# Batch 0's token sums by plain loads and three additions, its values in the input's order of heads, and a new table of ranks

## The chip, the cores and the metric

The kernel runs on one core of one Trainium2 chip. The metric is the device time of one execution in microseconds (us). The kernel before took 570.07 us, the median of three runs (569.68 to 573.22). The engines are named as the profile names them: PE multiplies matrices, PEld is its loading of weights, DVE is the vector engine, ACT the scalar engine, POOL the third one (GpSimd), SP issues most of the transfers between HBM and the core's memory.

## The reference

Inputs q, k and v have 8 batches, 8 heads, 576 tokens and 64 values per head. Each head's attention is the sum of two parts; its output goes, heads side by side, as x of [576, 512] per batch into a gated network. The core of it:

```python
q_d = q.reshape(B, H, Sd, factor, D).mean(axis=3)      # factor 4, k_d and v_d alike
out_up = np.repeat(sm_attn(q_d, k_d, v_d), factor, axis=2)
mask = np.abs(pos[:, None] - pos[None, :]) < factor
out_local = np.matmul(softmax(np.where(mask, scores, -1e9)), v)
x = out_up + out_local
h = np.maximum(x @ w_in, 0.0)
u, v = h[..., :d_ff // 2], h[..., d_ff // 2:]
v_n = (v - mu) / np.sqrt(var + 1e-06)
v_s = np.einsum('ts,bsd->btd', w_spatial, v_n) + b_spatial[None, :, None]
return (u * v_s) @ w_out
```

## The kernel before, in words

**Attention.** A batch has four pairs of heads; 32 pairs in all. Each pair goes through two attentions. The local one works in ten windows of 64 tokens: scores S on PE (line 873; on some pairs PE also adds the mask, line 866, on the others DVE does, line 886), maximum (889, or 895 where the mask is in already), subtraction (892 or 901), exponential on ACT (937), total (904), inverse (907, 908), multiplication by it ("norm", 941, on DVE or POOL), transposes T on PE (949), and AV, the product with the values (1060). The other one works on sums of four neighbouring tokens: two sums of q and k (844 and 847, on DVE or POOL), scores Sd (920), maximum, exponential, norm (974), transposes Td, and AVd (1040 for batch 0, 1049 for the others), the product with the token sums of v. The two are added into x (1070, 1072).

**The token sums of v.** The host lays v out as four quarters per batch, each 72 partitions by 1024 floats, one for each place in a group of four tokens. `load_down` loads the first quarter by SP (761) into the tile "tv" and lets POOL issue three transfers that add the others in memory (763).

**The values.** `load_v` loads a pair's ten windows in three transfers (775 and twice 777): the even blocks as they are, the odd blocks with the two heads swapped between the halves of the partitions. So in odd blocks the rows of a head lie in the other half, and in `views` and `values` the pieces of odd blocks are taken crosswise (`r = h ^ (blk % 2)`). AV's output rows always lie in the head's own half.

**The network.** Batch 0 (`FULL = 1`, "whole") is multiplied in plain 32-bit form, with the weights made from their 64-bit bits on DVE (lines 626 to 641; tiles mba to mbd for V, mbe to mbh for U); the other batches as pairs of 16-bit numbers, high and low part. Per batch: five V pieces (PE, line 1125 for batch 0, 1129 after that), then relu, statistics, scaling and the split into "vh"; eight U pieces (1191, 1196); a bound over U (`bound`: a transpose at line 569, the maximum on DVE at 572, a matmul at 575 that spreads it, the scale on DVE at 580 to 586); the spatial product SP with the split w_spatial (1218), the gate on DVE (1235), and the product O with w_out (1255). Each spatial product waits for the matmul that spreads the bound of U (`after=[known]`).

**The scale of w_spatial.** SP loads its rows first (611), ACT takes absolute values and row sums (724), PE adds the columns (740), DVE takes the maximum over the columns (743, tile "sw"), and the scale follows; the split of w_spatial and the scales of U come from it.

**What sets the order.** Every piece of work is an operation of the class `Plan`, with an engine, an estimated duration, the tiles that it reads and writes and a rank from the table ORDER. `Plan.run` walks through time and, for the engine that is free first, takes among the operations that can start within NEAR nanoseconds the one of lowest rank (PE keeps its tile shape where the rank is at most STAY behind). `Way` with the strings of ON says which engine does a kind of operation for each pair. Each engine then runs its list strictly in order, and so does each engine's queue of transfers. `warm` puts idle matmuls (1306) where PE would stand idle in the first 110 us.

Of the kernel before, what the change touches and what calls it, by code (L numbers as in the profile page):

```python
# [1351 lines left out]
```

## Time and profile before

| what | value |
|---|---|
| median of three runs | 570.07 us (569.68 to 573.22) |
| profiled execution | 572.09 us, span 570.3 us, mean granted clock 0.976 |
| PE busy | 547.1 us (96%) |
| DVE busy | 449.1 us (79%) |
| ACT busy | 358.5 us (63%) |
| POOL busy | 139.0 us (24%) |
| chain that ended last | PE 82%, DVE 10%, DMA 4%, ACT 2% |
| batch 0: first whole V, first spatial product | 53.64 us, 99.37 us |
| batch 1: first split V | 132.56 us |

The span is the time from the first to the last instruction of the profiled execution, and 1.79 us lie around it; this execution was 2.02 us above the median. The busy share is a mean over stages with different limits, so what an engine is worth has to be read by stage: the beginning, in which inputs come in and batch 0's attention runs on its own; batch 0's network beside batch 1's attention; and then the even part, in which each batch's network runs beside the next batch's attention. A duration in a row is that of one instruction, or of several that overlap (x2, x40), and an idle time in brackets is what its engine waited before it.

### The profile page before, as it was taken

How to read it: one execution, taken by the hardware profiler on the slowest of the kernel's cores; microseconds unless marked ns; L12 is line 12 of the kernel's file. 1: busy time of each engine (PE TensorE's matmuls, PEld its weight loads, DVE VectorE, ACT ScalarE, POOL GpSimd, SP SyncE). 2: the span in 40 equal slices, each digit the busy share in tenths (PEclk: the TensorE clock that was granted, in tenths of full speed). 3: DMA queues.
4: the chain of work that ended last, by engine and by line, in shares of the span. 5: the costliest groups of instructions: out<-in, count | busy, mean ns of one | idle time of the engine just before them, and what ended most of it. 6: DMA issues, size and time to landing. Idle time of an engine off the chain costs nothing.

```text
span 570.3 us, 15614 instructions
## 1 busy us (share of the span) xinstructions
PE 547.1 (96%) x6307; PEld 368.4 (65%) x6307; DVE 449.1 (79%) x1227; ACT 358.5 (63%) x913; POOL 139.0 (24%) x162
## 2 busy tenths in 40 slices
PE   5778799999999999999999999999999999999997
PEld 3446357866677567766678566766767756766573
DVE  5899989997989679886789798898969787832550
ACT  3758777765875578555766776657675666544422
POOL 4414331211421224101520054001610162001400
PEclk9758999999999999999999999999999999999999
DMA  9999834214550444415432336332450301000102
GB/s 241 264 259 285 196 66 120 94 35 142 105 144 25 148 99 96 124 38 173 69 105 70 127 93 135 109 113 87 109 139 8 114 33 39 21 1 18 50 7 92
DMA packets 40467, 59.76 MB, mean 105 GB/s; under 512 B 4042, under 2 KB 27210, under 8 KB 40396
## 3 DMA queue, kind: packets, MB, share of 16 engines
q1 hardware_dynamic: 38092, 51.69, 31.3%
q0 software_dynamic: 2304, 7.08, 7.6%
q8 instruction: 49, 0.80, 0.6%
q14 instruction: 22, 0.18, 0.1%
HBM read 46.57 MB, written 9.44 MB: 98 GB/s over the span
## 4 chain that ended last, share of the span: by engine, by line
PE 82%; DVE 10%; DMA 4%; ACT 2%; issue 1%; SPq 0%; POOL 0%; DVEq 0%; POOLq 0%; ACTq 0%
PE pma L1255 5%; PE pmc L1255 5%; PE pmd L1218 4%; PE pma L1196 4%; PE pma L1218 4%; PE pmb L1218 4%; PE pmc L1218 4%; PE pmb L1196 4%; PE pma L1129 4%; PE pmc L1129 4%; PE pmd L1255 3%; PE pmb L1255 3%; PE pmd L1129 3%; PE pmb L1129 3%; PE pmd L1196 3%; PE paa L1060 2%
## 5 line engine op out<-in xcount | busy, mean ns | idle before, releaser
L1218 PEld LDWEIGHTS <-vha 128*128 128x128 f16 x768 | 73.6, 98 | 19.5
L1196 PEld LDWEIGHTS <-win 128*128 128x128 f16 x672 | 64.8, 98 | 18.4
L941 POOL TENSOR_TENSOR sb<-sb,smb 128x640 f32<-128x640 f32 x12 | 16.4, 1366 | 74.3 <-DVE smb L908 63.9
L1255 PEld LDWEIGHTS <-more 128*128 128x128 f16 x192 | 18.5, 98 | 20.8
L1255 PEld LDWEIGHTS <-g 128*128 128x128 f16 x192 | 18.3, 98 | 20.8
L1218 PE MATMUL pmd<-wsp,vha 128*128 128x320 f16 (+1 forms) x192 | 27.5, 292 | 0.0
L1218 PE MATMUL pma<-wsp,vha 128*128 128x256 f16 (+1 forms) x192 | 26.2, 286 | 0.0
L1160 POOL TENSOR_TENSOR stb<-stb,mhalf 128x1 f32<-128x1 f32 (+1 forms) x13 | 9.7, 743 | 67.3 <-DVE stb L1141 67.3
L1218 PE MATMUL pmb<-wsp,vha 128*128 128x256 f16 (+1 forms) x192 | 25.5, 282 | 0.0
L1218 PE MATMUL pmc<-wsp,vha 128*128 128x256 f16 (+1 forms) x192 | 25.5, 282 | 0.0
L941 POOL TENSOR_TENSOR sa<-sa,sma 128x640 f32<-128x640 f32 x7 | 9.3, 1334 | 48.3 <-DVE sma L908 42.5
L1160 POOL TENSOR_TENSOR stc<-stc,mhalf 128x1 f32<-128x1 f32 (+1 forms) x13 | 9.2, 707 | 45.8 <-DVE stc L1141 45.7
L1255 PE MATMUL pmc<-wo,g 128*128 128x512 f16 x72 | 16.5, 379 | 0.0
L1160 POOL TENSOR_TENSOR sta<-sta,mhalf 128x1 f32<-128x1 f32 (+1 forms) x14 | 9.5, 681 | 26.7 <-DVE sta L1141 24.8
L978 DVE SCALAR_TENSOR_TENSOR eh<-eda,smda,eh 128x144 f16<-128x144 f32 x42 | 15.8, 440 | 0.1
L763 POOL DMA_DIRECT2D tv<-v_dram x12 | 11.5, 955 | 16.4 <-DMA tv<-v_dram 16.4
L1129 PEld LDWEIGHTS <-xa 128*128 128x128 f16 x84 | 8.2, 98 | 9.9
L904 DVE TENSOR_REDUCE smb<-sb 128x10 f32<-128x640 f32 x16 | 12.9, 809 | 1.3 <-ACT sb L937 1.3
L844 POOL TENSOR_TENSOR suma<-qka 128x576 f32<-128x576 f32 x5 | 6.8, 1370 | 29.1 <-DVE sma L904 16.9
L937 ACT ACTIVATE sb<-sb 128x640 f32<-128x640 f32 x16 | 11.8, 735 | 3.3 <-DVE sb L901 3.1
L1255 PE MATMUL pma<-wo,more 128*128 128x512 f16 x60 | 13.8, 379 | 0.0
L1255 PE MATMUL pmc<-wo,more 128*128 128x512 f16 x60 | 13.8, 379 | 0.0
(1025 smaller groups left out, 1719.7 us busy)
## 6 DMA issues: line engine op xcount, KB each, us to landing
qka<-qk_dram SPq DMA_DIRECT2D x16, 576.0 KB
qkb<-qk_dram SPq DMA_DIRECT2D x16, 576.0 KB, 5.1
tv<-v_dram POOLq DMA_DIRECT2D x12, 288.0 KB, 5.9
wst<-v_dram POOLq DMA_DIRECT2D x12, 288.0 KB, 4.6
stg<-w_in_dram SPq DMA_DIRECT2D x6, 512.0 KB, 6.1
out_dram<-rowb SPq DMA_DIRECT2D x8, 256.0 KB, 2.4
out_dram<-rowe SPq DMA_DIRECT2D x7, 256.0 KB
out_dram<-rowa SPq DMA_DIRECT2D x7, 256.0 KB
```

The source lines that it names most:

```text
L763: plan.op("POOL", 850, lambda r=r: nc.gpsimd.dma_start(t.ap, v4[b, r], accum_op=ALU.add), w=[t], rank=rank + 2.0 + 0.3 * r, kb=288, name="tv")
L844: side(s1).tensor_tensor(sb.ap.rearrange("p x (g r) -> p x g r", r=2), x[:, :, :, :2], x[:, :, :, 2:], op=ALU.add)
L904: nc.vector.tensor_reduce(sm.ap, s.ap, axis=AX.X, op=ALU.add)
L937: exp_of.append(plan.op("ACT", 643, lambda: nc.scalar.activation(s.ap, s.ap, AF.Exp, scale=1.0 / 8.0), w=[s], rank=R["E"], name="exp"))
L941: plan.op(nm, 0, lambda: side(nm).tensor_tensor(s.ap, s.ap, sm.ap[:, :, None].broadcast_to([P, NW, 64]), op=ALU.mult), r=[sm], w=[s], rank ...
L978: nc.vector.scalar_tensor_tensor(eh.ap[:, a, :, 1], ed.ap[:, a, :], smd.ap[:, a:a + 1], eh.ap[:, a, :, 0], op0=ALU.mult, op1=ALU.subtract)
L1060: nc.tensor.matmul(pv.ap[h * 64:h * 64 + 64, c:c + QB[w + 1] - QB[w]], vb.ap[k, w], pT.ap[k, blk, q0:q0 + QB[w + 1] - QB[w]], start=True, ...
L1129: nc.tensor.matmul(ps.ap, xs[c].ap[:, i, t * P:(t + 1) * P], win[:, c, j, FF:], start=(c == 0 and (i, j) == (0, 0)), stop=(c == NC - 1 and ...
L1160: plan.op("POOL", 830, lambda: nc.gpsimd.tensor_tensor(st.ap[:r, 8:9], st.ap[:r, 8:9], mhalf[:r], op=ALU.pow), w=[st], rank=rank - EVICT, ...
L1196: nc.tensor.matmul(ps.ap[:, :n], win[:, c, i, ft * P:(ft + 1) * P], xs[c].ap[:, j, HA[h]:HA[h + 1]], start=(c == 0 and (i, j) == (0, 0)), ...
L1218: nc.tensor.matmul(ps.ap[:, :n], vh.ap[:, c, i, fs], wsp[:, c, j, hs], start=(c == 0 and (i, j) == (0, 0)), stop=False)
L1255: nc.tensor.matmul(ps.ap, g.ap[:, c, i, k:k + P] if t < NT else gt.ap[:, c, i], wo[:, c, j, :], start=(c == 0 and (i, j) == (0, 0)), stop= ...
```

## The change

Three things change for batch 0, and the order of everything.

The token sums of batch 0: the four quarters are loaded by SP with plain transfers into storage that batch 0's network uses only later (two into the tile "vh", two into the nine tiles "us"), and three additions of 72x1024 make the sum, two on DVE and one on POOL. The other batches keep the adding transfers.

The values of batch 0: one transfer per pair, heads unswapped. `views` and `values` take odd blocks straight where the batch is whole. Each head's rows then lie in the same half at AV's input and output.

The table ORDER is replaced (some 1,600 numbers), with NEAR 121 for 131.8 and STAY 12.56 for 5.08, and the strings of ON: among others one "shrink" of the weights more on DVE, more early masks on PE (letters T), other places for sums and norms. The durations that the planner counts with change to 450 for a load of batch 0's values and 1150 for an AV of batch 0.

```diff
-    583.50, 595.07, 582.09, 590.75, 523.79, 633.37, 571.27]
-NEAR = 131.8
-STAY = 5.08
+    548.47, 513.63, 618.17, 559.57]
+NEAR = 121
+STAY = 12.56
...
-ON = {"shrink": "AAAAAAADA",
-      "sum": "DPDPDPDDPDDDPDPDDPDDDDDDPDDDPDDP",
-      "mask": "DDDTTTDTDDTTDTDDDDTTDTDDDDDDTD",
+ON = {"shrink": "AAADAAADA",
+      "vsum": "DDP",
+      "sum": "DPPPDPDDDDDDPDPDDPPDDDDDDDPDPDDP",
+      "mask": "DTTTTTTTDDTDDTDDDDTTDTDTDDDDTD",
...
-    places("u", 9, [P, HN], F32)
+    us = const.tile([P, 9, HN], F32, name="us")
+    plan.tag("u", [us[:, i] for i in range(9)])
+    quarters = [a[:72, i * 2 * FF:(i + 1) * 2 * FF].rearrange("p (j d) -> p j d", j=NP)
+                for a in (vh.rearrange("p t i f -> p (t i f)").bitcast(F32), us.rearrange("p i t -> p (i t)")) for i in range(2)]
...
     def load_down(b):
+        if b < FULL:
+            for r in range(4):
+                plan.op("SP", 450, lambda r=r: nc.sync.dma_start(quarters[r], v4[b, r]), w=[("v4", r)], rank=0.0, kb=288, name="v4")
+            for i, (x, y) in enumerate(((0, 1), (2, 3), (0, 2))):
+                w = Way("vsum", i, P=("POOL", 2200, True), D=("DVE", 1135, True))
+                plan.op(w, 0, lambda w=w, x=x, y=y: side(w).tensor_tensor(quarters[x], quarters[x], quarters[y], op=ALU.add),
+                        r=[("v4", y)], w=[("v4", x)], rank=RANK["th"][0], name="vsum")
+            tv_of[b] = None
+            return
...
+            if b < FULL:
+                nc.sync.dma_start(vb.ap, vw[b, p])
+                return
...
-            sv = s.ap.rearrange("p (j h) k -> p h j k", h=2)[:, ::-1 if odd else 1, odd::2]
+            sv = s.ap.rearrange("p (j h) k -> p h j k", h=2)[:, ::-1 if odd and not whole else 1, odd::2]
...
-                r = h ^ (blk % 2)
+                r = h if whole else h ^ (blk % 2)
...
-            av = plan.op("PE", 675, values, r=[vb, pT], w=[pv], hold=[xf, x], after=after, rank=R["AV"], lag=PEL, mode="Q", name="AV")
+            av = plan.op("PE", 1150 if whole else 675, values, r=[vb, pT], w=[pv], hold=[xf, x], after=after, rank=R["AV"], lag=PEL, mode="Q", name="AV")
```

Three places of the order. First DVE ahead of the maximum over the columns of w_spatial (the tiles s and mx are scores and their maxima, ed and md belong to the attention on sums). Before:

```order
L925 TENSOR_SCALAR mxdb<-mxdb 128x3
L974 TENSOR_TENSOR eda<-eda,smda 128x432
L889 TENSOR_REDUCE mxb<-sb 128x10
L904 TENSOR_REDUCE sma<-sa 128x10
L892 TENSOR_TENSOR sb<-sb,mxb 128x640
L907 TENSOR_SCALAR sma<-sma 128x10
L908 RECIPROCAL sma<-sma 128x10
L961 TENSOR_SCALAR smdb<-smdb 128x3
L962 RECIPROCAL smdb<-smdb 128x3
L904 TENSOR_REDUCE smb<-sb 128x10
L907 TENSOR_SCALAR smb<-smb 128x10
L908 RECIPROCAL smb<-smb 128x10
L743 TENSOR_REDUCE sw<-pma 128x1
```

and now, where vh and us are the quarters:

```order
L907 TENSOR_REDUCE mxa<-sa 128x10
L913 TENSOR_REDUCE mxb<-pab 128x10
L919 TENSOR_TENSOR sb<-pab,mxb 128x2x3x64
L919 TENSOR_TENSOR sb<-pab,mxb 128x2x2x64
L910 TENSOR_TENSOR sa<-sa,mxa 128x640
L770 TENSOR_TENSOR vh<-vh 72x1024
L770 TENSOR_TENSOR us<-us 72x1024
L941 TENSOR_REDUCE mxdb<-pmd 128x2
L942 TENSOR_REDUCE mxdb<-pmb 128x1
L943 TENSOR_SCALAR mxdb<-mxdb 128x3
L922 TENSOR_REDUCE sma<-sa 128x10
L922 TENSOR_REDUCE smb<-sb 128x10
```

Two additions of quarters, and the maximum and subtraction of the second pair straight from its scores, which carry the mask already, now stand there; the maximum over the columns (750) comes ten rows later.

Second SP's queue at the start (qk are q and k of a pair, wst the rows of w_spatial, va to vd the values). Before:

```order
L837 DMA qka<-qk_dram 128x1152
L837 DMA qkb<-qk_dram 128x1152
L611 DMA xfa<-bsp_dram 2x576
L761 DMA tv_125<-v_dram 72x1024
L611 DMA wst<-wT_dram 128x576 x4
L611 DMA wst<-wT_dram 64x576 x2
L775 DMA va<-vw_dram 128x3x128
L777 DMA va<-vw_dram 64x2x128 x2
L837 DMA qka<-qk_dram 128x1152
L775 DMA vb<-vw_dram 128x3x128
L777 DMA vb<-vw_dram 64x2x128 x2
```

and now:

```order
L855 DMA qka<-qk_dram 128x1152
L855 DMA qkb<-qk_dram 128x1152
L767 DMA vh<-v_dram 72x1024
L618 DMA xfa<-bsp_dram 2x576
L767 DMA vh<-v_dram 72x1024
L767 DMA us<-v_dram 72x1024 x2
L618 DMA wst<-wT_dram 128x576 x4
L618 DMA wst<-wT_dram 64x576 x2
L855 DMA qka<-qk_dram 128x1152
L791 DMA va<-vw_dram 128x640
L791 DMA vb<-vw_dram 128x640
L791 DMA vc<-vw_dram 128x640
L791 DMA vd<-vw_dram 128x640
L618 DMA stg<-w_in_dram 128x1024 x2
L855 DMA qkb<-qk_dram 128x1152
```

Four quarters stand ahead of w_spatial where one stood; the values take one issue each and come one behind another, ahead of w_in (stg) and of the next q and k.

Third PE between the last U piece and the first spatial product of batch 0 (the rows that load weights of the ident and cross matrices are left aside). Before:

```order
L1191 MATMUL pma<-xd,mbh 128x320
L569 MATMUL pmd<-ident,sw 4x128
L873 MATMUL pab<-qka 64x64 x20
L575 MATMUL pmd<-sw,one 128x1
L569 MATMUL pmc<-ident,uta 8x128
L866 MATMUL paa<-mask_b,mask_a 64x320
L873 MATMUL paa<-qkb 64x64 x20
L1049 MATMUL pma<-pdTa,th_126 64x144
L575 MATMUL pmc<-uta,one 128x1
```

and now:

```order
L1209 MATMUL pmb<-xd,mbh 128x320
L576 MATMUL pma<-ident,sw 4x128
L1067 MATMUL pmc<-pdTa,th_126 64x144
L576 MATMUL pmd<-ident,uta 8x128
L582 MATMUL pma<-sw,one 128x1
L967 MATMUL pab<-ident,sa 128x128 x5
L938 MATMUL pmb<-kdb 64x144 x2
L938 MATMUL pmc<-kdb 64x144 x2
L938 MATMUL pmb<-kdb 64x144 x2
L582 MATMUL pmd<-uta,one 128x1
L1078 MATMUL paa<-probTb,vf 64x60 x2
L1236 MATMUL pma<-wsp,vh 128x256
```

A transpose of probabilities (967), an Sd (938) and half an AV (1078) now stand ahead of the first spatial product, with two spreads of maxima (582) between them.

## Rows read from the trace of the kernel before

**Rows 1.** The page: busy time of each engine (first row), and the span in 40 equal slices, each digit the busy share of PE in tenths; DMA is the mean busy share of the 16 DMA engines in the same slices:

```profile
PE 547.1 (96%) x6307; PEld 368.4 (65%) x6307; DVE 449.1 (79%) x1227; ACT 358.5 (63%) x913; POOL 139.0 (24%) x162
...
PE   5778799999999999999999999999999999999997
...
DMA  9999834214550444415432336332450301000102
```

**Rows 2.** The windows by stage: start and end, length, then busy time (and instructions) of PE, PEld, DVE, ACT and POOL, PE's granted clock, the DMA share and GB/s:

```profile
0.00:20.00 20.00, 12.78 (x138) 7.25 (x139) 12.38 (x32) 9.47 (x29) 10.49 (x32) 0.89 0.98 240
20.00:53.40 33.40, 26.23 (x463) 18.79 (x461) 31.76 (x74) 24.84 (x64) 9.71 (x10) 0.71 1.01 275
53.40:99.37 45.97, 41.83 (x249) 24.52 (x249) 43.01 (x117) 34.32 (x88) 13.36 (x14) 0.96 0.59 135
99.37:132.56 33.19, 33.19 (x449) 23.17 (x446) 31.49 (x96) 24.01 (x58) 5.18 (x4) 1.00 0.31 97
132.56:571.00 438.44, 433.02 (x5017) 294.70 (x5015) 330.48 (x912) 265.81 (x675) 100.24 (x103) 1.00 0.31 83
```

**Rows 3.** The timeline of PE: start, duration, engine, line and operation, out<-in with shapes, how many run together, and in brackets the idle time before and what ended it:

```profile
53.64 1.02 PE L1125 MATMUL pmd<-mba,xa 128*128 128x512 f32 x2
...
68.76 0.77 PE L949 MATMUL paa<-ident,sb 128*128 128x128 f32 x5 [3.59 <-POOL sb L941]
...
70.09 2.07 PE L1125 MATMUL pmb<-mba,xa 128*128 128x512 f32 x2
...
99.37 1.48 PE L1218 MATMUL pmd<-wsp,vha 128*128 128x256 f16 x12
...
132.56 0.81 PE L1129 MATMUL pmc<-win,xe 128*128 128x512 f16 x3
```

**Rows 4.** The timeline of DVE, the same columns:

```profile
19.20 0.46 DVE L743 TENSOR_REDUCE sw<-pma 128x1 f32<-128x288 f32 x1
...
45.90 0.82 DVE L895 TENSOR_REDUCE mxa<-pab 128x10 f32<-128x640 f32 x1 [0.51 <-PE pab L873]
46.82 0.89 DVE L901 TENSOR_TENSOR sa<-pab,mxa 128x384 f32<-128x384 f32 x2
...
52.58 0.70 DVE L1070 TENSOR_TENSOR xd<-pab,dnb 128x232 f32<-128x232 f32 x2
...
71.67 0.74 DVE L602 SCALAR_TENSOR_TENSOR win<-mba,sw,win 128x512 f16<-128x512 f32 x1
...
75.59 0.28 DVE L572 TENSOR_REDUCE sw<-pmc 4x1 bf16<-4x128 f32 x1 [0.92 <-PE pmc L569]
...
95.40 0.28 DVE L572 TENSOR_REDUCE sw<-pmd 4x1 bf16<-4x128 f32 x1 [0.43 <-PE pmd L569]
...
97.22 0.86 DVE L886 TENSOR_TENSOR sa<-pab,mask 128x384 f32<-128x384 f32 x2
98.00 0.27 DVE L572 TENSOR_REDUCE uta<-pmc 8x1 bf16<-8x128 f32 x1
98.20 0.80 DVE L889 TENSOR_REDUCE mxa<-sa 128x10 f32<-128x640 f32 x1
```

**Rows 5.** The adding transfers of batch 0 on POOL in the timeline, then the landing times of line L763 up to 36 us, then the first AVd on PE in the timeline:

```profile
9.11 1.02 POOL L763 DMA_DIRECT2D tv<-v_dram  x1 [1.69 <-DMA tv<-v_dram]
...
27.08 0.84 POOL L763 DMA_DIRECT2D tv<-v_dram  x1 [0.56 <-DMA tv<-v_dram]
...
DMA to landing us min/median/max: 7.2/8.1/8.8
...
37.13 0.76 PE L1040 MATMUL pmd<-pdTa,tv 72*64 72x144 f32 x4
```

**Rows 6.** The timeline of POOL (one row) and of DVE: instructions alone and beside POOL:

```profile
19.26 1.54 POOL L941 TENSOR_TENSOR sb<-sb,smb 128x640 f32<-128x640 f32 x1
...
20.04 1.39 DVE L844 TENSOR_TENSOR suma<-qka 128x576 f32<-128x576 f32 x1 [0.19 <-DMA qka<-qk_dram]
...
43.13 0.75 DVE L844 TENSOR_TENSOR suma<-qka 128x576 f32<-128x576 f32 x1
43.79 0.16 DVE L961 TENSOR_SCALAR smdb<-smdb 128x3 f32<-128x3 f32 x1
...
44.08 0.43 DVE L847 TENSOR_TENSOR kda<-suma 128x288 f32<-128x288 f32 x1
...
95.98 1.12 DVE L961 TENSOR_SCALAR smda<-smda 128x3 f32<-128x3 f32 x1
...
99.60 0.81 DVE L892 TENSOR_TENSOR sa<-sa,mxa 128x640 f32<-128x640 f32 x1
```

**Rows 7.** The timeline of SP's queue (issues of transfers, the duration is that of issuing) and one row of ACT:

```profile
2.36 4.25 SPq L611 DMA_DIRECT2D wst<-wT_dram  x6
...
8.81 1.31 SPq L777 DMA_DIRECT2D va<-vw_dram  x2
...
22.05 1.07 SPq L611 DMA_DIRECT2D stg<-w_in_dram  x2
...
12.04 0.68 ACT L724 ACTIVATE wsp<-wst 128x576 bf16<-128x576 f32 x1
```

**Rows 8.** The timeline of PE: AV of the first pair and the larger piece of the last pair of batch 0:

```profile
21.70 1.11 PE L1060 MATMUL paa<-probTa,va 64*64 64x60 f32 x40
...
50.57 0.81 PE L1060 MATMUL pab<-probTb,vd 64*64 64x60 f32 x38
```

More of the change, by code (lines that the diff above doesn't have):

```diff
@@ L61, in __init__ @@
     def __init__(self, kind, i, **ways):
-        s = ON[kind]
+        s = ON.get(kind, "D")
         self.kind, self.i, self.ways = kind, i, ways
@@ L422 @@
 MB = 8
-ON = {"shrink": "AAAAAAADA",
-      "sum": "DPDPDPDDPDDDPDPDDPDDDDDDPDDDPDDP",
-      "mask": "DDDTTTDTDDTTDTDDDDTTDTDDDDDDTD",
-      "norm": "PPPPDPPPDPDPPDDDDPPDDPDPDPDDP",
-      "normd": "DPPAPAAADPAPAAAPPADAAPDADAAADDDA",
-      "vlo": "DPDDDPDDDDDPDPDDPDPDPDPPDPDPPDPPDDDP"}
+ON = {"shrink": "AAADAAADA",
+      "vsum": "DDP",
+      "sum": "DPPPDPDDDDDDPDPDDPPDDDDDDDPDPDDP",
+      "mask": "DTTTTTTTDDTDDTDDDDTTDTDTDDDDTD",
+      "norm": "PPPPDPPPDPDDDDDPDDDPDPDPPPDPPD",
+      "normd": "DPPAPAAAAPAAPAAPAADADADAAADDDA",
+      "vlo": "DPDDDPPDDDDPPDDDPPPDPPDPDDPPDDPPPDDPPDP"}
 @with_exitstack
@@ L537, in tile_kernel @@
     places("xtail", 2, [P, NC, 2, TAIL], F16)
-    places("vh", 1, [P, NT, 2, FF], F16)
+    vh = const.tile([P, NT, 2, FF], F16, name="vh")
+    plan.tag("vh", [vh])
     places("vt", 1, [P, FF], F16)
@@ L757, in load_down @@
     def load_down(b):
+        if b < FULL:
[7 more added lines that the diff above has]
+            return
         t = tv_of[b] = plan.buf("tv")
         rank = NP * b + RANK["tv"][min(b, 2)]
-        plan.op("SP", 450, lambda: nc.sync.dma_start(t.ap, v4[b, 0]), w=[t], after=exp_of[NP * b - NP + 1:][:1] if b else (), rank=rank, kb=288, name="tv0")
+        plan.op("SP", 450, lambda: nc.sync.dma_start(t.ap, v4[b, 0]), w=[t], after=exp_of[NP * b - NP + 1:][:1], rank=rank, kb=288, name="tv0")
         for r in range(1, 4):
@@ L777, in go @@
                 nc.sync.dma_start(dst[(1 - h) * 64:(2 - h) * 64, 1::2], src[h * 64:h * 64 + 64, 1::2])
-        plan.op("SP", 1500, go, w=[vb], after=exp_of[NP * b - NP + p:][:1] if b else (), rank=NP * b + 0.2 * p + RANK["vload"][min(b, 2)], kb=320, name="v")
+        plan.op("SP", 450 if b < FULL else 1500, go, w=[vb], after=exp_of[NP * b - NP + p:][:1] if b else (), rank=NP * b + 0.2 * p + RANK["vload"][min(b, 2)], kb=320, name="v")
         if b < FULL:
@@ L1039, in values_d @@
                 for kc, n in enumerate(KEYS):
-                    nc.tensor.matmul(pw.ap[h * 64:h * 64 + 64, :G], tv.ap[:, p, (2 * kc + h) * D:(2 * kc + h + 1) * D], t[:n, kc, :, h, :],
+                    nc.tensor.matmul(pw.ap[h * 64:h * 64 + 64, :G], quarters[0][:, p, (2 * kc + h) * D:(2 * kc + h + 1) * D], t[:n, kc, :, h, :],
                                      start=(kc == 0), stop=(kc == 1))
@@ L1075, in finish @@
         def finish(*after):
-            av = plan.op("PE", 675, values, r=[vb, pT], w=[pv], hold=[xf, x], after=after, rank=R["AV"], lag=PEL, mode="Q", name="AV")
+            av = plan.op("PE", 1150 if whole else 675, values, r=[vb, pT], w=[pv], hold=[xf, x], after=after, rank=R["AV"], lag=PEL, mode="Q", name="AV")
             avd = plan.op("PE", 450 if whole else 240, values_d if whole else values_h,
-                          r=[*((tv,) if whole else (th_of[b].sub(0),)), pdT.sub(0), pdT.sub(1)], w=[pw], hold=[dn], after=[av] if after else (), rank=R["AVd"], lag=PEL, mode="H", name="AVd")
+                          r=[*((("v4", 0),) if whole else (th_of[b].sub(0),)), pdT.sub(0), pdT.sub(1)], w=[pw], hold=[dn], after=[av] if after else (), rank=R["AVd"], lag=PEL, mode="H", name="AVd")
             if after:
```

242 rows, old and new, of the table ORDER are left out of this document.

## The prediction

> **What bounds the kernel now.** I read the page first, then the windows by stage, then the timeline of PE and DVE. PE is busy for 547.1 of 570.3 us, and its 40 slices show where the rest went: the first four [rows 1]. The windows [rows 2] say it in numbers. From 132.56 us on, PE works 433.02 of 438.44 us at a granted clock of 1.00, so nothing but PE counts there. From 20 to 53.4 us it works 26.23 of 33.40 at a clock of 0.71, and DVE 31.76: here DVE is the engine that has no room. From 53.4 to 99.37 (the first matmul of the spatial product) DVE works 43.01 of 45.97, PE 41.83. So from about 20 us to the first spatial matmul DVE's order sets the pace; from there on PE does; the first whole V of batch 0 is at 53.64, the first spatial product at 99.37, the first split V of batch 1 at 132.56 [rows 3].
>
> The profiled execution took 572.09 us, span 570.3 and 1.79 around it; the median of three is 570.07, that is 2.02 less. I work on the profiled times and take 2.02 off at the end.
>
> **What is removed.** The chain for batch 0's token sums: one SP load, then three adding transfers issued by POOL, the first at 9.11 and the last at 27.08, each waiting for the one before, which land 7.2 to 8.8 us after issue; the first AVd can start at 37.13 [rows 5]. Three issues of 0.84 to 1.02 us leave POOL, which had 9.71 us of work in 33.4 [rows 2]: worth nothing there. That x of the first head pair now comes some 9 us earlier is also worth nothing by itself, since DVE went on with other work meanwhile (31.76 of 33.40).
>
> **What is added.** (1) Three quarters more at the head of SP's queue, 72x1024 floats each, 0.885 MB in all. At 240 GB/s, the rate of the first window [rows 2], that puts the weights of the spatial product, issued behind them (2.36 in [rows 7]), up to 3.7 us later. ACT's absolute-value passes over them begin at 12.04, column sums on PE follow, and DVE's maximum over these is at 19.20 [rows 4, 7]. Between the passes and the maximum lies other work of ACT and PE that need not wait with them, so I take 2.2 of the 3.7: the maximum at 21.4. Bounds: 0.9 (the DVE work newly ahead of it) and 3.7.
> (2) Three additions of 72x1024, two on DVE and one on POOL. On DVE 128x576 takes 0.75 and 128x640 0.81 [rows 6]; the slope gives 1.15 for 1024, in proportion it is 1.30. I take 1.14 each, 2.3 together. On POOL 128x640 took 1.54 [rows 6]: 2.2 to 2.5 for the one. POOL's own time is free.
> (3) Values in one transfer per head pair, where SP issued three, 1.31 us for the latter two [rows 7]. The DMA engines are full there (0.98, 1.01 in [rows 2]), so SP's issue time is not what is short: nothing.
> (4) Batch 0's AV without the swap of heads in odd blocks. Rows of AV are 1.11 us early and, at the full clock, 0.81 [rows 8]. PE idles 7.2 us in that window, and before the last x (DVE, 52.58) its AV (50.57 to 51.38) has 1.2 us to spare: nothing, if an AV grows by less than that. Beside this stands the Trainium skill, "TensorEngine Tiling (Array Packing)", Tile-to-Partition Mapping: a 64x64 tile is fixed by its input half and its output half, four in all, so that heads never swapped use two of the four; AV would take up to twice as long, and with 0.8 us on the path the gain would be 0.3 us instead of what follows.
>
> **What moves.** The table of ranks lays all engines anew. Steady state has PE work alone, with the same instructions, and it cannot gain: 0, with 1 us either way. What counts is the road to the first spatial matmul.
> On DVE I take the maximum for the bound of batch 0's U (on "uta", 98.00 in [rows 4]) as the mark, since the spatial products wait for the matmul that spreads it; the first follows it by 1.37 us. By the order printed above, ahead of it now stand two token additions (+2.3), four more maxima on scores that carry the mask already (4 x 0.82) and their subtractions (4 x 0.89 the pair), for three fewer masks (3 x 0.86), two fewer maxima over a masked tile (2 x 0.80) and subtractions (2 x 0.81), one total (0.80, as a maximum) and the larger part of one x (0.70) more, one weight product (0.74) and one second sum (0.43) less [rows 4, 6]; small pieces come to some 0.6 more. That is 4.3 by durations; consecutive starts lie some 0.08 closer than durations, so 4.0.
> Against it, waits that DVE had and whose cause goes: 0.64 where a sum ran beside POOL's normalization (1.39 against 0.75 [rows 6]), 0.96 on a 128x3 instruction (1.12 against 0.16 [rows 6]), 0.51, 0.92 and 0.43 for PE [rows 4]. Together 3.46, for places that the new order takes apart. New is the later maximum at the start, 2.2 less the 0.9 of work: 1.3. So the mark comes at 98.00 + 4.0 - 3.46 + 1.3 = 99.9 and the first spatial matmul at 101.3.
> Then PE: of what lay between it and the first split V, one T (0.77 [rows 3]), one AV (0.81 [rows 8]), one AVd (0.7 as four matmuls of it in [rows 5]) and one Sd (0.5, estimated from its share of these) now stand ahead of it, 2.8, and some 0.2 for changes between tile shapes. 33.2 becomes 30.2, the split V starts at 131.5 and not 132.56. The gain is 1.1 us: 572.09 - 1.1 = 571.0, less 2.02: **569.0 us**.
> That PE itself does not stop it: with the first whole V at 56.4 instead of 53.64 (one more head's scores, mask, T and AV lie ahead, 2.3, and the sign pass of the first weight block 0.5 later), without the 3.59 us hole at 68.76 and with the V pieces behind it as fast as at 53.64 (two in 1.02, and not in 2.07; the next two alike, 1.8 in all) [rows 3], plus 1.2 of moved pieces, PE would be there at 98.0. It waits for DVE there, late in U's bound.
>
> **The rivals.**
> - *PE alone sets the start* (faster). If DVE loses 3 us less than I think (of the 12.2 it idles up to 99.37 [rows 2]), the spatial product starts at 98.0, the split V at 128.2: 4.4 gained, **565.7**; with the tail 1 us better, 564.7. For it: the hole at 68.76 was a wait for POOL, which the new order puts elsewhere. Against it: 4 us more DVE work on that road.
> - *The parked maximum* (slower). DVE runs in order, and behind the maximum stand all its score passes. If the quarters cost the full 3.7 us and none of the 3.46 us of old waits is won back, the mark is at 98.0 + 4.0 + (3.7 - 0.9) = 104.8, the split V at 136.4, 3.8 later: **573.9**. It decides against the change as soon as DVE loses 1.1 us more than in my sum, since that is the whole gain. For it: DMA is full for 50 us [rows 1], and the later weights w_in (issued 22.05 [rows 7]) queue behind the same bytes. Against it: the three adding transfers moved the same 0.885 MB before 35 us.
> - *POOL's addition holds DVE.* The row: a DVE sum that began beside POOL's normalization ended 0.6 us after it (19.26+1.54 = 20.80; 20.04+1.39 = 21.43 [rows 6]), as if it had begun at its end. POOL's 72x1024 addition may so cost DVE up to its own 2.2 us: 569.0 + 2.2 = **571.2**. The Trainium skill, "SBUF — State Buffer", Who interferes with whom, has this as a rule (two inputs in SBUF against a POOL instruction that reads SBUF: the later one is blocked until the end); these rows agree.
> - *Nothing moves*: the start is absorbed where DMA is full and both orders reach 132.56 alike: **570.1**.
>
> **How the numbers follow.** Forecast 0.45 (568 to 570.5 with its small terms), PE alone 0.22, the parked maximum 0.15, POOL's hold 0.10, nothing moves 0.08. The range takes in PE alone and the parked maximum up to its full price, and leaves out mixtures beyond: 564.0 to 574.0. One per cent, about what a measurement here can tell, is 5.7 us: 564.4 and 575.8. Below the first lies the better half of "PE alone" with a better tail or a second hole closed, 0.13; above the second the parked maximum with w_in late as well, 0.06; between them 0.81.
>
> **What would show it.** Right: AVd of the first pair before 30 us; the columns' maximum near 21.4; first whole V near 56.4 with no hole of over 2 us behind it; first spatial matmul near 101.3 with PE waiting for DVE just before; the first split V near 131.5; no change from there to the end. PE alone would show as a spatial start near 98 with DVE early. The parked maximum would show as DVE idle for 3 us or more ahead of it, and the first whole V past 58; POOL's hold as a DVE row of over 2 us beside the addition. The prediction is wrong if the steady part is not of equal length, since I gave the table of ranks no effect there.

## The result and the profile after

The changed kernel took 576.00 us, the median of five executions (575.86 to 576.43), against 570.07 before (569.68 to 573.22): 1.0087 of the time before, 95% interval 1.0065 to 1.0109. It is slower, by 3.7 to 6.2 us. The profiled execution took 575.86 us, span 573.7, 0.14 below its median; the one of before had been 2.02 above its own, so the two profiles lie only 3.8 us apart.

The windows of the changed kernel, with the same borders as [rows 2] (the last one is longer by 4 us):

```profile
0.00:20.00 20.00, 10.06 (x132) 5.25 (x133) 13.98 (x28) 8.93 (x26) 9.38 (x29) 0.93 0.92 288
20.00:53.40 33.40, 25.59 (x383) 19.01 (x382) 27.00 (x67) 21.87 (x61) 15.05 (x15) 0.78 0.79 226
53.40:99.37 45.97, 41.73 (x378) 25.19 (x378) 45.11 (x118) 35.31 (x86) 11.87 (x12) 1.00 0.68 183
99.37:132.56 33.19, 32.57 (x404) 22.98 (x403) 32.23 (x103) 24.05 (x65) 4.66 (x4) 1.00 0.14 39
132.56:575.00 442.44, 436.54 (x5033) 296.16 (x5030) 326.64 (x914) 271.07 (x688) 95.11 (x101) 1.00 0.31 83
```

From 20 to 53.4 us DVE now works 27.00 us where it had 31.76. That is the window in which it had no room, and it now has 6.4 us without work.

PE's timeline: AV of the last pair, the first whole V, the first piece of the fourth, the spread ahead of the spatial product, that product, the first split V:

```profile
54.41 1.30 PE L1078 MATMUL paa<-probTb,vd 64*64 64x60 f32 x38
...
62.22 1.12 PE L1143 MATMUL pmb<-mba,xa 128*128 128x512 f32 x2
...
76.62 1.13 PE L1143 MATMUL pmb<-mba,xa 128*128 128x512 f32 x2 [1.37 <-ACT rowd L1165]
...
103.68 0.16 PE L582 MATMUL pma<-sw,one 4*128 4x1 bf16 x1 [0.54 <-DVE sw L579]
...
106.05 1.16 PE L1236 MATMUL pma<-wsp,vh 128*128 128x256 f16 x9
...
135.86 0.81 PE L1147 MATMUL pmc<-win,xe 128*128 128x512 f16 x3
```

The first whole V is 8.6 us later than in [rows 3] (62.22 for 53.64), the first spatial product 6.7 us (106.05 for 99.37), the first split V 3.3 us (135.86 for 132.56). From there to the end of the span it is 437.8 us, and before it was 437.7. All of the loss arises ahead of the first spatial product, and PE gives half of it back between that and the split V. PE's last wait before that product is for DVE (0.54 <-DVE at 103.68).

DVE's timeline, with the two additions (12.13, 13.26), the column maximum (24.02), the last sign pass over V's weights (61.03) and the mark (104.35), and POOL's timeline beside it:

```profile
12.13 1.22 DVE L770 TENSOR_TENSOR vh<-vh 72x1024 f32<-72x1024 f32 x1
13.26 1.21 DVE L770 TENSOR_TENSOR us<-us 72x1024 f32<-72x1024 f32 x1
...
15.09 1.83 DVE L943 TENSOR_SCALAR mxdb<-mxdb 128x3 f32<-128x3 f32 x1
...
19.34 1.23 DVE L979 TENSOR_SCALAR smdb<-smdb 128x3 f32<-128x3 f32 x1
...
24.02 0.46 DVE L750 TENSOR_REDUCE sw<-pmd 128x1 f32<-128x288 f32 x1 [2.93 <-PE pmd L747]
...
25.50 0.16 DVE L587 COPY sw<-pma 128x1 f32<-128x1 f32 x1 [0.84 <-PE pma L582]
...
27.02 0.82 DVE L913 TENSOR_REDUCE mxb<-paa 128x10 f32<-128x640 f32 x1 [0.74 <-PE paa L891]
...
48.74 0.46 DVE L941 TENSOR_REDUCE mxda<-pmc 128x2 f32<-128x288 f32 x1 [1.11 <-PE pmc L938]
...
49.45 1.61 DVE L943 TENSOR_SCALAR mxda<-mxda 128x3 f32<-128x3 f32 x1
...
61.03 0.67 DVE L648 SCALAR_TENSOR_TENSOR mbd<-rowc,mbd 128x512 int32<-128x512 int32 x1
...
104.35 0.27 DVE L579 TENSOR_REDUCE uta<-pmd 8x1 bf16<-8x128 f32 x1
```

```profile
14.56 2.34 POOL L770 TENSOR_TENSOR vh<-vh,us 72x1024 f32<-72x1024 f32 x1 [5.99 <-DVE us L770]
19.11 1.44 POOL L959 TENSOR_TENSOR sa<-sa,sma 128x640 f32<-128x640 f32 x1 [2.21 <-DVE sma L926]
...
49.58 1.45 POOL L862 TENSOR_TENSOR suma<-qkb 128x576 f32<-128x576 f32 x1
```

Three things are to be read here. The column maximum came at 24.02 us where it had been at 19.20 [rows 4], after 2.93 us of waiting for PE, and 0.84 and 0.74 us follow. Second, instructions on 128x3 that take 0.16 us elsewhere [rows 6] took 1.83, 1.23 and 1.61 us. Each ends with a POOL instruction: 15.09+1.83 = 16.92 and 14.56+2.34 = 16.90; 19.34+1.23 = 20.57 and 19.11+1.44 = 20.55; 49.45+1.61 = 51.06 and 49.58+1.45 = 51.03. In the last of the three, DVE's row begins 0.13 us before POOL's and is held all the same. Third, the addition on POOL is the longest of these. Behind its victim, the scaled maximum "mxdb", stand the exponentials on ACT, and behind them ACT's last passes over w_spatial:

```profile
17.01 0.38 ACT L975 ACTIVATE edb<-pmd,mxdb 128x144 f32<-128x144 f32 x1 [1.82 <-DVE mxdb L943]
...
19.43 0.68 ACT L731 ACTIVATE wsp_lb<-wst 64x576 bf16<-64x576 f32 x1
```

PE stands idle meanwhile, and its granted clock is at the lower of its two levels (1.2 and 2.4 GHz) when it goes on. PE's timeline, and the window from 20 to 25 us in the order of [rows 2], where 0.50 is the clock:

```profile
19.57 0.56 PE L1013 MATMUL pmc<-ident,eda 112*72 112x112 f32 x2 [5.03 <-ACT wsp L731]
...
20.00:25.00 5.00, 5.00 (x23) 2.99 (x21) 1.67 (x6) 0.99 (x4) 4.43 (x5) 0.50 1.04 394
```

### The profile page after: what moved, and what is told of

It reads as the page before. It is cut to its first block, busy times and chain, and to the rows that moved or that the text cites. A ratio compares the mean times of both kernels' runs of the same rounds, so it can differ in the third digit from the quotient of the medians.

```text
span 573.7 us, 15659 instructions
## 1 busy us (share of the span) xinstructions
PE 546.5 (95%) x6325; PEld 368.6 (64%) x6325; DVE 445.0 (78%) x1226; ACT 361.2 (63%) x921; POOL 136.1 (24%) x158
## 4 chain that ended last, share of the span: by engine, by line
PE 84%; DVE 12%; ACT 3%; issue 1%; POOL 1%; POOLq 0%; ACTq 0%
PE pma L1273 6%; PE pmd L1236 5%; PE pma L1214 5%; PE pma L1236 4%; PE pmc L1214 4%; PE pmb L1236 4%; PE pmd L1273 4%; PE pmc L1273 4%; PE pmc L1147 4%; PE paa L1078 3%; PE pmb L1273 3%; PE pmb L1147 3%; PE pma L1147 3%; PE pmb L1214 3%; PE pmc L1236 3%; PE pmd L1147 3%
## 5 line engine op out<-in xcount | busy, mean ns | idle before, releaser
L1236 PEld LDWEIGHTS <-vh 128*128 128x128 f16 x768 | 73.4, 98 | 19.1
L1236 PE MATMUL pmd<-wsp,vh 128*128 128x320 f16 (+1 forms) x240 | 33.4, 289 | 0.0
L1236 PE MATMUL pma<-wsp,vh 128*128 128x256 f16 (+1 forms) x204 | 27.7, 285 | 0.0
L1246 ACT CAST g<-us 128x256 f16<-128x256 f32 x32 | 12.9, 402 | 19.9 <-DVE us L1253 19.6
L1236 PE MATMUL pmb<-wsp,vh 128*128 128x256 f16 (+1 forms) x180 | 24.1, 283 | 0.0
L1236 PE MATMUL pmc<-wsp,vh 128*128 128x320 f16 (+1 forms) x144 | 19.6, 286 | 0.0
L1273 PE MATMUL pma<-wo,g 128*128 128x512 f16 x84 | 19.3, 379 | 0.0
L1246 ACT CAST more<-us 128x256 f16<-128x256 f32 x32 | 12.8, 403 | 9.4 <-DVE us L1253 9.3
L1250 DVE TENSOR_TENSOR more<-us,more 128x256 f16<-128x256 f32 x32 | 13.4, 422 | 4.8 <-ACT more L1246 4.7
L1250 DVE TENSOR_TENSOR g<-us,g 128x256 f16<-128x256 f32 x32 | 13.3, 418 | 2.5 <-ACT g L1246 2.4
## 6 DMA issues: line engine op xcount, KB each, us to landing
qka<-qk_dram SPq DMA_DIRECT2D x16, 576.0 KB
qkb<-qk_dram SPq DMA_DIRECT2D x16, 576.0 KB
```

The costliest lines, as they stand in the source:

```text
L1236: nc.tensor.matmul(ps.ap[:, :n], vh.ap[:, c, i, fs], wsp[:, c, j, hs], start=(c == 0 and (i, j) == (0, 0)), stop=False)
L1246: nc.scalar.copy(part(tail, 0), u.ap[:, i:j])
L1250: nc.vector.tensor_sub(part(tail, 1), u.ap[:, i:j], part(tail, 0))
L1273: nc.tensor.matmul(ps.ap, g.ap[:, c, i, k:k + P] if t < NT else gt.ap[:, c, i], wo[:, c, j, :], start=(c == 0 and (i, j) == (0, 0)), stop= ...
```

## The experiments

In every run each engine keeps the list that the planner laid out for the kernel in question, and the edit is made on the finished list, so that nothing moves but what is named. The "old order" is the one of the kernel before. Medians in us; the ratio is to the kernel before, run beside it on the same chip (median 570.7 beside runs 1 to 4, 570.8 beside 5 to 8, 571.1 beside 9 to 12). The last five columns are read from PE's and DVE's timeline of the one profiled execution, which need not lie at the median: it is 2.0 us above it in the kernel before, 2.8 below in run 2, 0.7 below in run 3, 0.8 to 1.1 above in runs 5, 6, 7 and 9 and 0.9 below in run 11; in the others within 0.3. Columns of two runs compare only as far as that allows.

| run | median | ratio (95%) | column maximum | first whole V | mark on DVE | first spatial product | first split V |
|---|---|---|---|---|---|---|---|
| before | 570.07 | 1 | 19.20 | 53.64 | 98.00 | 99.37 | 132.56 |
| changed kernel | 576.00 | 1.0087 (1.0065 to 1.0109) | 24.02 | 62.22 | 104.35 | 106.05 | 135.86 |
| 1 all parts, old order | 578.20 | 1.0124 (1.0086 to 1.0162) | 24.77 | 59.20 | 103.50 | 104.67 | 138.05 |
| 2 values only, old order | 571.55 | 1.0007 (0.9985 to 1.0029) | 18.50 | 51.50 | 94.20 | 95.63 | 129.00 |
| 3 changed, no additions | 572.54 | 1.0029 (1.0009 to 1.0049) | 20.73 | 58.05 | 100.20 | 101.90 | 131.70 |
| 4 changed, ACT's passes early | 574.67 | 1.0083 (1.0060 to 1.0105) | 21.84 | 61.19 | 103.34 | 105.05 | 134.85 |
| 5 loads only, old order | 575.33 | 1.0083 (1.0067 to 1.0099) | 22.17 | 57.52 | 101.93 | 103.11 | 136.56 |
| 6 quarters behind, old order | 575.99 | 1.0088 (1.0069 to 1.0108) | 18.42 | 57.32 | 101.74 | 102.98 | 136.36 |
| 7 changed, additions in the gap | 576.85 | 1.0102 (1.0072 to 1.0133) | 23.51 | 63.85 | 106.00 | 107.70 | 137.51 |
| 8 changed, third addition on DVE | 575.22 | 1.0082 (1.0063 to 1.0101) | 23.32 | 61.60 | 103.76 | 105.46 | 135.26 |
| 9 new order, no sums | 571.14 | 1.0001 (0.9986 to 1.0015) | 19.97 | 58.89 | 101.05 | 102.75 | 132.56 |
| 10 changed, heads swapped | 574.58 | 1.0060 (1.0041 to 1.0080) | 24.26 | 62.25 | 103.38 | 105.08 | 134.88 |
| 11 sums on PE | 576.91 | 1.0121 (1.0072 to 1.0170) | 19.04 | 63.40 | 104.32 | 106.02 | 135.82 |
| 12 sums on PE, quarters behind | 580.15 | 1.0162 (1.0131 to 1.0193) | 21.15 | 66.63 | 107.93 | 109.63 | 139.44 |

**Run 1: the parts in the old order.**

```diff
 SP:   q,k  q,k  bsp
-      first quarter into tv
+      four quarters into vh and us
       w_spatial ...
 DVE: ... inverse of edb's sums
+      vsum(0, 1)  vsum(2, 3)
       total of the second pair ...
 POOL: sum1 of the fourth pair
-      adding transfer 3
+      vsum(0, 2)
```

> The kernel before with its own order on every engine, and all parts of the change but the new tables: four plain loads of the quarters where the first one stood, two additions on DVE just ahead of the second pair's total, the third on POOL where the last adding transfer was issued, values in one transfer per pair, heads unswapped. Theory A (the parts cost the time: additions, POOL holding DVE, AV on two tiles): 573 to 576 us. Theory B (the new order costs it, the parts alone are cheap): 569.5 to 571.5 us, first spatial product within 1.5 us of the 99.4 of before.

Measured 578.2 us. It goes as theory A says, and 2.2 us beyond its range. The parts in the old order are 2.2 us above the changed kernel by the medians; the intervals of the two ratios overlap, so that the new table wins some of their cost back is likely and not shown.

**Run 2: the values only.**

```diff
+            if b < FULL:
+                nc.sync.dma_start(vb.ap, vw[b, p])
+                return
...
-                r = h ^ (blk % 2)
+                r = h if whole else h ^ (blk % 2)
```

> The kernel before, with batch 0's values in one transfer per pair and the heads unswapped, nothing else. AV of the last pair of batch 0 should go from 0.81 to about 1.3 us at the full clock, as it did in the changed kernel. If AV's length were on the path (theory A in part), 571 to 572.5 us; if it is hidden by DVE, 570 us within 0.6.

AV of the last pair in PE's timeline of this run:

```profile
48.10 1.27 PE L1063 MATMUL pab<-probTb,vd 64*64 64x60 f32 x38
```

It took 1.27 us where [rows 8] have 0.81, and the time did not move beyond its interval (1.0007, 0.9985 to 1.0029): no cost of it is seen in the old order, though the interval would hide one of up to 1.7 us.

**Run 3: no additions.**

```diff
-                plan.op(w, 0, lambda w=w, x=x, y=y: side(w).tensor_tensor(quarters[x], quarters[x], quarters[y], op=ALU.add), ...)
```

> The changed kernel without its three additions (batch 0's token sums then hold one quarter of the four). On DVE 2.4 us of additions and the 1.7 us by which a 128x3 instruction was held beside POOL's addition are gone. If DVE's road to the spatial product is one chain, all of it reaches the end: 571.9 to 573 us, first spatial product at 102 to 103. If the wait for the column maximum of w_spatial takes it up (that maximum depends on ACT and PE): 575 to 576 us and that wait grows from 2.9 to 5 us or more.

572.54 us, the mark at 100.20 for 104.35. By the ratios 3.3 us of the change's 5 us go with the additions. The two additions (1.22+1.21 us by their rows, 1.14 and 1.13 from start to start) and the 1.66 us of hold come to nearly the same 4.15 us, but that is in part luck, for the timelines show another sum. Before the additions run 3 is 0.4 us ahead already. At the column maximum it is 3.29 ahead, since waits of 0.90 and 1.23 us for ACT take up a part of what the additions and the holds leave; the wait there stays (2.72 us), as ACT's passes also come earlier. Behind it the lead grows by another 1.2 us:

```profile
20.00:25.00 5.00, 4.73 (x116) 3.70 (x115) 3.78 (x14) 3.21 (x5) 3.03 (x3) 1.00 1.02 379
...
22.51 0.82 DVE L913 TENSOR_REDUCE mxb<-paa 128x10 f32<-128x640 f32 x1
```

This maximum stands at 27.02 in the changed kernel, after waits for PE of 0.84 and 0.74 us; here the first is 0.25 and the second is gone. PE's granted clock from 20 to 25 us is 1.00 here and 0.50 there. So a part of these 4.15 us is PE's clock in the two executions, and not a price of the additions that can be counted on: run 9, without additions, has 0.51 in this window.

**Run 4: ACT's passes ahead.**

```diff
 ACT:  w_spatial rows 1, 2
-      exponentials of the second pair
       w_spatial rows 3, 4, 5
+      exponentials of the second pair
 PE:  -transposes of the first pair's sums
       column sums
+      transposes of the first pair's sums
```

> The changed kernel with three passes of ACT over w_spatial ahead of the second pair's exponentials, the columns on PE ahead of the first transposes, and the inverse that waits for these exponentials behind the scale of w_spatial on DVE; all else in place. Theory A' (DVE parked 2.9 us at the column maximum is what was lost): maximum at 21.5 to 22 instead of 24.02, 573.3 to 574 us. Theory B (the order ahead of V and U, not the start): the time is taken up before the first whole V, 575.5 to 576 us. No late weights: if the quarters had delayed the rows of w_spatial, ACT would now wait for them by more than 1 us.

The maximum came at 21.84, 2.2 us earlier, as expected, but only 1.0 us of that is left at the first spatial product. The time is 574.67, 1.3 below the changed kernel by the medians, while the ratios (1.0083 and 1.0087) do not tell the two apart. So the trace shows the park at the maximum as a part of the loss, of which less than half reaches the spatial product. The edit also gives less than it was meant to. The column sums are written into the tile "pmd", which two of the second pair's exponentials read, and these now stand behind ACT's passes:

```profile
18.48 1.84 PE L747 MATMUL pmd<-wsp,near 128*128 128x288 bf16 x7 [4.33 <-ACT edb L975]
```

ACT waited 0.45 us for rows of w_spatial, so in the new order the bytes are not what holds them in the first place.

**Runs 5 and 6: bytes and additions apart, in the old order.** Run 5 is run 1 without the additions; run 6 is:

```diff
 SP:   q,k  q,k  bsp
-      first quarter into tv
       w_spatial ...
+      four quarters into vh and us
 DVE: ... scale of w_spatial ...
+      vsum(0, 1)  vsum(2, 3)  vsum(0, 2)
       low part of w_spatial ...
```

> The kernel before in its own order, with the four plain loads ahead of w_spatial and the values unswapped, without any addition (batch 0's token sums hold one quarter). Theory C (the three quarters more ahead of w_spatial make its rows late; ACT, PE and DVE then stand still for them): ACT waits 3 to 4.5 us for rows of w_spatial as in the run with all parts, the column maximum comes at 22 to 23, 573.5 to 575 us. Theory D (the additions on DVE and their clash with POOL are the cost, the bytes are free): 570 to 571.5 us.

> The kernel before in its own order, the four plain loads behind the rows of w_spatial, three additions on DVE behind the scale of w_spatial, values unswapped. Theory C: the column maximum is back at 18.5 to 19.5 us; what is left is 3.5 us of additions on DVE, less about 2 us in which DVE was held beside POOL's issues of the adding transfers: 571 to 573 us. Theory D: the same kernel costs the full additions, 573.5 us and more. Under neither does it beat the kernel before by 1 us or more, since DVE's work on that road only grows.

ACT's timeline in run 5, two of its passes over w_spatial:

```profile
13.45 0.69 ACT L728 ACTIVATE wsp<-wst 128x576 bf16<-128x576 f32 x1 [2.08 <-DMA wst<-wT_dram]
...
16.97 0.68 ACT L728 ACTIVATE wsp<-wst 128x576 bf16<-128x576 f32 x1 [1.38 <-DMA wst<-wT_dram]
```

The loads, with the values unswapped as in run 2, cost 4.5 us (575.33 for 570.8, 0.3 above the range of theory C): ACT waits 2.08 and 1.38 us for the rows behind them, and the column maximum is 3.7 us later than in run 2 (22.17 for 18.50), which is the full price of 0.885 MB at 240 GB/s. Theory C holds for the bytes. But run 6, with the weights first again, misses its 571 to 573 us by 3. DVE's timeline:

```profile
18.42 0.46 DVE L747 TENSOR_REDUCE sw<-pma 128x1 f32<-128x288 f32 x1
...
20.49 0.76 DVE L854 TENSOR_TENSOR suma<-qka 128x576 f32<-128x576 f32 x1 [1.43 <-DMA qka<-qk_dram]
...
23.82 1.21 DVE L766 TENSOR_TENSOR vh<-vh 72x1024 f32<-72x1024 f32 x1
24.95 1.21 DVE L766 TENSOR_TENSOR us<-us 72x1024 f32<-72x1024 f32 x1
26.20 2.06 DVE L766 TENSOR_TENSOR vh<-vh,us 72x1024 f32<-72x1024 f32 x1
```

The maximum is back at 18.42. Now q and k of the third pair are late (1.43 us), and the third addition takes 2.06 us in place of 1.21. So theory D has its share too: the additions take 4.4 us of DVE, from 23.82 to 28.26, and bytes moved out of the way of one load stand in the way of the next.

**Runs 7 and 8: where the additions stand.** Run 7 moves all three, on DVE, to just ahead of the column maximum; run 8 gives only the third to DVE, in its place:

```diff
-side(w).tensor_tensor(quarters[x], quarters[x], quarters[y], op=ALU.add)
+nc.vector.tensor_tensor(quarters[x], quarters[x], quarters[y], op=ALU.add)
```

> The changed kernel with its three additions all on DVE just ahead of the column maximum, where DVE idles 2.9 us, and none on POOL. Theory D' (where the additions stand, and POOL's hold on DVE, cost 3.4 us): the exponentials of the second pair start 3 us earlier, the maximum comes at 21.5 to 22.5, 573 to 574.5 us. If the additions cost only their own time wherever they stand: 575.5 to 577 us.

> The changed kernel with the third addition on DVE behind the second, all else in place. If POOL's addition holds DVE (the 128x3 instruction of 1.83 us), that instruction takes 0.17 us again and the start comes 0.4 to 0.6 us earlier: 575.2 to 576 us. If the 1.83 us have another cause, it stays long and the kernel is 1.1 us slower, 577 us.

DVE's timeline of run 8 and of run 7:

```profile
14.93 0.17 DVE L943 TENSOR_SCALAR mxdb<-mxdb 128x3 f32<-128x3 f32 x1
15.00 1.21 DVE L770 TENSOR_TENSOR vh<-vh,us 72x1024 f32<-72x1024 f32 x1
```

```profile
18.46 1.90 DVE L770 TENSOR_TENSOR vh<-vh 72x1024 f32<-72x1024 f32 x1
20.29 1.21 DVE L770 TENSOR_TENSOR us<-us 72x1024 f32<-72x1024 f32 x1
21.53 2.05 DVE L770 TENSOR_TENSOR vh<-vh,us 72x1024 f32<-72x1024 f32 x1
23.51 0.44 DVE L750 TENSOR_REDUCE sw<-pmd 128x1 f32<-128x288 f32 x1
```

Run 8 shows the hold by itself: with no POOL instruction beside it the same 128x3 instruction takes 0.17 us and not 1.83. The third addition (1.21 us) cost less on DVE, where it is work, than on POOL, where it cost DVE 1.66 us; the mark is 0.6 us earlier and the time 575.22 us, both as expected, though the intervals of the two ratios overlap. Run 7, at 576.85, falls into the range for additions that cost their own time wherever they stand: they took 1.90, 1.21 and 2.05 us, and the first whole V is 1.6 us later than in the changed kernel. Its four executions lie far apart: two at a mean granted clock of 0.976, the profiled one among them, took 577.8 and 578.3 us, two at 0.985 574.5 and 575.9, so whether it is slower than the changed kernel stays open. The gap at the maximum is there only while nothing fills it; what delays V in this run beyond the longer additions I did not trace.

**Runs 9 and 10: the order and the values.** Run 9 is run 3 without the loads of quarters 2 to 4; run 10 is the changed kernel with the three transfers and the swapped heads of before.

> The changed kernel without its additions and without the loads of the second to fourth quarter (batch 0's token sums hold one quarter): the new order, the values unswapped, the bytes at the start as before. Theory C' (bytes and additions of the sums are the whole loss, the new order is no worse than the old one): 569 to 571.3 us, first spatial product at 98.5 to 100.5. Theory E (the new order has 4 us more DVE work ahead of the first spatial product and costs time by itself): 572.3 us and more, hardly below the 572.5 of the changed kernel without additions.

> The changed kernel with batch 0's values as before (three transfers per pair, heads of odd blocks swapped), all else in place. AV of a pair should fall from about 1.3 to 0.8 us at the full clock. If AV lies on the path in the new order: 574 to 575 us; if DVE hides it, 575.5 to 576.5 us.

AV of the last pair in run 10, where the changed kernel has 1.30 at 54.41, and one row each of DVE and of POOL, where the changed kernel has 1.61 at 49.45 and 1.45 at 49.58:

```profile
53.15 0.83 PE L1075 MATMUL paa<-probTb,vd 64*64 64x60 f32 x38
...
49.42 0.17 DVE L940 TENSOR_SCALAR mxda<-mxda 128x3 f32<-128x3 f32 x1
...
49.92 1.44 POOL L859 TENSOR_TENSOR suma<-qkb 128x576 f32<-128x576 f32 x1
```

Run 9 takes 571.14 us, 1.0001 of before. The new table by itself, with the unswapped values and without the adding transfers, neither wins nor loses, so theory C' holds in the time and theory E falls. Its mark stands at 101.05 and its first spatial product at 102.75, 2 us past the range of theory C': PE gives those 3 us back behind that product, as the forecast said it would. So the sums, bytes and additions together, are the whole loss. Their split is less sure. By the medians the bytes add 1.4 us from run 9 to run 3 and the additions 3.5 from run 3 to the changed kernel. But in the two profiled executions run 3 is 0.9 us ahead of run 9 at the first whole V, so the 1.4 us are not found in the traces. PE's clock from 20 to 25 us is 0.51 in that of run 9 and 1.00 in that of run 3, with an idle time of 2.1 us ahead in both (up to 16.76 and 16.23 us), so the idle time alone does not tell which of the two it will be.

Run 10 is 1.4 us below the changed kernel by the medians and 1.0 by the mark; the intervals of the two ratios overlap. By the rows this 1.0 us is not the length of AV as such: at 48.7 us DVE is level in the two runs (0.03 us apart, after run 10 had lain 0.3 behind; its wait there is 0.74 us for 1.11, which is the most that the shorter AV can have given), and what run 10 wins is the 128x3 instruction behind it, which ends before POOL's sum begins and takes 0.17 us where the changed kernel has 1.61.

**Runs 11 and 12: no additions at all.** AVd takes all four quarters on PE; run 12 also puts the quarters behind w_spatial and has the order of run 4.

```diff
-                    nc.tensor.matmul(pw.ap[...], quarters[0][:, p, ...], t[:n, kc, :, h, :], start=(kc == 0), stop=(kc == 1))
+                    for r in range(4):
+                        nc.tensor.matmul(pw.ap[...], quarters[r][:, p, ...], t[:n, kc, :, h, :],
+                                         start=(kc == 0 and r == 0), stop=(kc == 1 and r == 3))
```

> The changed kernel without additions; AVd of batch 0 takes all four quarters into one accumulation, so that each of its four AVd has 32 matmul records in place of 8 and 2 us more of PE. If PE's idle time at the start covers them, the time is that without additions, 572 to 573.2 us; if they fall on the path between AV and x (4 x 2 us, one of them for certain ahead of the last x), 574 to 578 us.

> As the run before it, and the four quarters behind the rows of w_spatial in SP's queue, ACT's passes over w_spatial ahead of the second pair's exponentials, column sums ahead of the first transposes. Theory C' (what waits for w_spatial's scale at the start reaches the end): column maximum at 18.5 to 20 us and 1.5 to 2.5 us less than the run before it; 570 to 572 us if PE hides the longer AVd. If only the additions count, the same time as the run before it within 0.6 us.

DVE's timeline of run 12:

```profile
21.15 0.46 DVE L750 TENSOR_REDUCE sw<-pmd 128x1 f32<-128x288 f32 x1 [3.43 <-PE pmd L747]
...
31.79 0.71 DVE L1089 TENSOR_TENSOR xa<-pab,dna 128x232 f32<-128x232 f32 x2 [2.43 <-ACT dna L1100]
```

576.91 and 580.15 us: the sums on PE are not hidden. DVE stands 2.43 us ahead of the first x, waiting for ACT's copy of the longer AVd. Run 12 goes against its expectation by far: the maximum came at 21.15, later than the 19.04 of run 11, and the time got worse by 3.2 us. The trace of the profiled execution shows a part of the reason, as in run 4:

```profile
17.78 2.08 PE L747 MATMUL pmd<-wsp,near 128*128 128x288 bf16 x8 [3.42 <-ACT edb L975]
```

The column sums waited for the exponentials after all, PE stood idle for 3.42 us, and its granted clock from 20 to 25 us was 0.50, where run 11 has 1.00. DVE's next maximum over scores is at 25.25 us, and at 20.82 in run 11. No version here beats the kernel before.

## Why the prediction was wrong

The forecast was 569.0 us, in a range up to 574.0, with 0.06 for slower by over 1%. The measured 576.0 lies above the range and above 575.8, in the part that was given 0.06.

**What held.** The loss or gain was to be decided on the road to the first spatial product, with DVE setting the pace: so it is. From 49 us to the mark DVE idles 0.45 us in all; PE idles 2.1 from the first whole V to that product, 0.54 of it for DVE, so it has little more room. From that product to the split V the forecast had 30.2 us, and the trace has 29.81; the tail is of equal length. The additions took 1.22 and 1.21 us on DVE and 2.34 on POOL (1.14 and 2.2 to 2.5 forecast). The first AVd came before 30 us:

```profile
28.89 0.72 PE L1058 MATMUL pmd<-pdTa,vh 72*64 72x144 f32 x8
```

It is worth nothing, as said: DVE reaches its first x without a wait before (39.03) and after (30.96).

**The step that failed** is "waits that DVE had and whose cause goes", 3.46 us that the new order was to win back. They were written off one by one from rows of before, and no wait of the new order was put against them except 1.3 us at the start. Up to the mark, DVE's waits in brackets sum to 11.9 us in the timeline of after and to 10.0 in that of before; what instructions took beyond the shortest of their kind (those over 0.15 us beyond it) sums to 5.8 and 4.1. So the waits grew by 3.6 us where the forecast had them shrink by 2.2. That is 5.8 us of difference, more than the mark's error (104.35 for 99.9, 4.45 us); the work was then some 1.3 us less than the 4.0 that were counted.

Run 9 shows the step by itself. Without the sums the forecast's own terms put the mark at 98.0 + 4.0 - 2.3 - 3.46 = 96.2; it came at 101.05, with waits of 12.3 us and 4.5 us of longer instructions already. The forecast had the new order win 4.8 us, 1.8 up to the mark and 3.0 on PE behind it, and the sums take 3.6 of that back. Measured, PE's part came (3.4 us), the mark's did not (3.05 later instead of 1.8 earlier), so that the order wins nothing (1.0001), and the sums cost about 5 us (1.0087).

**Sizes within it.** The maximum was put at 21.4 us, between bounds of 20.1 and 22.9 (0.9 and 3.7 us); it came at 24.02, outside. In the old order the full 3.7 us were paid (run 5 against run 2). In the new one the bytes cost it only 0.8 us (19.97 to 20.73, runs 9 and 3), and the additions ahead of the second pair's maximum cost 3.3 (20.73 to 24.02), by one execution each. The forecast looked at the queue of transfers and not at the chain from the additions over the 128x3 instruction and ACT's exponentials to ACT's passes.

**POOL's addition** was said to be free in the sum, and a hold of up to 2.2 us on DVE stood as a rival with 0.10. The hold was 1.66 us, and run 8 shows its cause. Other work of POOL held two more such instructions (1.23 and 1.61 us above). The Trainium skill, "SBUF — State Buffer", Who interferes with whom, had more than the forecast used: it names the one-input scalar instructions beside the two-input ones as able to contend, under conditions that no run here tests. The trace agrees: a 128x3 one took 1.83 us beside POOL's addition and 0.17 without it.

**AV** was to cost nothing if it grew by less than 1.2 us; it grew by 0.46 to 0.49 at the full clock. In the old order run 2 shows no cost, within its interval. The Trainium skill's rule on four fixed tiles ("TensorEngine Tiling (Array Packing)", Tile-to-Partition Mapping) would allow up to twice the 0.81 us by the forecast's estimate, and 1.27 to 1.30 were measured. In the new order the rows leave at most 0.4 us to AV's length by itself; the 1.0 us of run 10 goes with a hold beside POOL.

**The rivals.** The parked maximum, with 573.9 us and a chance of 0.15, named the mechanism that came nearest, and its "none of the 3.46 us of old waits is won back" is what happened. In the trace its figures nearly came true: mark 104.8 (104.35 measured), first split V 136.4 (135.86). Its 573.9 is below the 576.0 mainly by the 2.02 us taken off. That the sizes fit is in part luck: it had the bytes at their full price and no hold, where the new order paid less for the bytes and more for the additions.

**The reference point.** 2.02 us were taken off because the profiled execution of before was that much above its median. The 24 executions of before beside runs 1 to 4 range from 569.2 to 574.2 us, those at a mean granted clock of 0.973 at 572.1 to 574.2, those at 0.985 to 0.988 at 569.2 to 571.2; the profiled one had 0.976. So the excess goes, at least in part, with PE's clock in that execution. The changed kernel's executions lie within 0.6 us of each other at 0.985, and taking the excess off its time too was 1 to 2 us too kind to the change: the profiled executions lie 3.8 us apart, the kernels 5.0 by the ratio and 5.9 by the medians.

## What to carry to other kernels

Work that an adding transfer does costs the compute engines little beside its issue (here three of 0.84 to 1.02 us on POOL); moved onto the engine that sets the pace it costs its full time, and moved onto POOL it can cost that engine as much again, as long as the one holds the other (1.66 us here for an addition of 1.21). Loads that were put ahead in a full queue made what stood behind them late by bytes over rate (3.7 us in run 5), and the bill came at the first instruction that waits for them in order, a maximum behind which DVE stood. When a new order is judged, old waits that vanish may be counted only together with the new ones, read from the new order at each place where an engine must wait for another.

## What was not expected of the hardware

A 128x3 instruction on DVE, 0.17 us alone, took up to 1.83 us because a 72x1024 addition ran on POOL; its end follows POOL's by 0.02 to 0.03 us in three places, beside POOL instructions of three sizes. And AV of batch 0, whose heads now stay in their own halves, took 1.6 times as long as with heads that cross over (1.30 for 0.81 us at the full clock), not twice.
